# A planned kernel of memory attention and a gated layer on one core: one block's loads issued earlier, casts, output stores and weight sums put elsewhere in the plan

## The chip, the core and the metric

The kernel runs on one core of one Trainium2 chip. The metric is the time of one execution on the device in microseconds. Beside it stand profiles: one execution recorded by the hardware profiler, with a span from the first to the last instruction. The engines are PE (TensorE), DVE (VectorE), ACT (ScalarE), POOL (GpSimd) and SP (SyncE, which issues the loads and stores); each works through its own queue in order.

## What is computed

Attention with a compressive memory, over 4 batches, 8 heads, 576 positions and 64 channels, and behind it a gated feed-forward layer on its 2304 x 512 result:

```python
local = softmax(scale * q @ k.T, causal) @ v
mem_out = (phi(q) @ M_prev) / (phi(q) @ z_prev + 1e-6)
x = (g * mem_out + (1 - g) * local)          # 2304 tokens x 512
gate = x @ w_gate                            # 512 -> 1536
out = (silu(gate) * (x @ w_val)) @ w_out     # 1536 -> 512
```

## The kernel before

Every product runs on fp32 data split in two parts: a high part, cast to fp32r by ACT (`...h`), and a low part, what is left of it, by DVE (`...l`). A product is then three matmuls (high x high, high x low, low x high).

The attention fills about the first 183 us and leaves its result in DRAM as `xdh` and `xdl`. The tokens are then taken as three blocks of 768 (`ORDER`, line 30). Each block is multiplied with the 12 slices of 128 columns (f = 0 to 11) of `w_gate` and `w_val`. Except for the first three slices of block one, a slice and a block together form a **unit**: Strassen's seven products p1 to p7 in the order of `STEPS` (line 37), each of six matmuls of 128 x 384. `chain` (line 869) holds what follows each product. The products go by turns into two PSUM banks (`ring`, line 737), and several add up in the same bank, so that a product two steps later has to wait until the bank was read: ACT copies p1, p6 and p7 out (`zp`, `zh`, `zv`; in blocks two and three `zpw` and `zvw`), and DVE adds to these when it reads p2, p5 and p4 (`zg`, `zv`, `zh`), with a SiLU on ACT behind p2 and p4. After p3, DVE forms the two results of the unit (`use`).

The seven products need sums of the four quarters of a block's input. `sums` (line 755) makes them: `begin` issues the loads of the first two quarters (`load(0)`, `load(1)`, each one DMA from `xdh` into `xr` or `yr` and one from `xdl` into `xm` or `xt`, `ym` or `yt`), `add(n)` adds high and low part on DVE and, for n = 0 and 1, issues the loads of quarter n + 2, and four more DVE instructions make the sums. Each load is told to wait for the DVE instruction that was the last in program order when it was written (line 766). For block two the tiles are called x, for block three y. `high` and `low` (lines 784 and 787) then split a sum, `yp7h` and `yp7l` for p7 of block three. Quarters needed unmixed are loaded by `direct` (line 749).

The weights come as 64-bit numbers and are unpacked in thirds (`third`, line 248) by ACT, POOL and DVE; `operands` (line 708) makes the sums of weights for the next unit: `tt` (DVE), `th` and `bh` (ACT), `tl` and `bl` (DVE). The last output products of block one (`lower`, line 804) run between the products of the following unit.

The order is written out by hand. `seven` (line 898) runs one unit: after product n come the entries of `plan[n]`, then, if n is in `away_at`, one entry of `leave`, then one `lower`. The entries of `leave` are `away` (line 814): ACT scales one finished bank of block one's output into a tile `pt` of the pool `tmp`, and SP stores it. PE, ACT, DVE and POOL keep program order (`queued`, line 83); DMAs are put in SP's queue by the framework's scheduler, by when their data and memory are ready.

The part around the change goes as follows:
- block one, f = 3 to 11, in the loop from line 947 (`left` is 11 - f);
- first lone unit (line 1019): block two, f = 11, with block one's last six `lower`s; three `away`s after n = 3, 5 and 6;
- second lone unit (line 1043): block two, f = 10; the splits of block three's sums are in its plan, and three `away`s after n = 0, 2 and 4;
- third lone unit (line 1055): block three, f = 10; sums of results that are kept for later (`some_sums`);
- the pools `xr3p` and `tmp` are released and `tp` is opened in their room (lines 1056 to 1059);
- fourth lone unit (line 1079): block three, f = 11; the operands for f = 0 are in its plan;
- then ten pairs of units, f = 0 to 9, in which blocks two and three take turns product by product (line 1131), and from line 1198 the output products of these two blocks.

`tees(r)` (line 1061) makes sums of `w_out` for the output products, six rounds: two loads into `w2` (called `w` in the trace), four subtractions on POOL into `tq` and a store to `tdr`. There are two `w2` and two `tq`. Round 0 is written in the fourth lone unit after n = 0, round 1 + f in pair f after n = 1; the pool `tp` is released at the pair behind the last round, and `p3a` is opened there.

Of the kernel before, what the change touches and what calls it, by code (L numbers as in the profile page):

```python
# [29 lines left out]
ORDER = (0, 768, 1536)  # L30
# [15 lines left out]
def attention_moe(ctx: ExitStack, tc: tile.TileContext, qt, kt_, v, m, beta, wg, wv, wo, out):  # L46
# [123 lines left out]
    xs = {p: [near.tile([128, 2, N2], F32R, name=f"x{p}{part}") for part in "hl"] for p in STEPS}  # L170
# [530 lines left out]
    xr3p = tc.alloc_tile_pool(name="xr3", bufs=1, side="right", reuse_waits="tile")  # L701
# [53 lines left out]
    def sums(t0, pool_, name, here=False):  # L755

        got = rot(pool_, f"{name}r", [128, 4, 2, N2], F32, 1)
        a21, a22, a11, a12 = (got[:, n] for n in range(4))
        s1, s = (rot(pool_, f"{name}{n}", [128, 2, N2], F32, 1) for n in "tm")
        two = (s, s1)  # L760
        mix = dict(p6=s, p7=a11, p5=s1, p3=a12)

        def load(n):
            for dst, src in ((got[:, n], xdh), (two[n % 2], xdl)):
                ld = SP.dma_start(dst, block(src, t0, *AT[n]))
                follow(ld, last[DVE], "the loads that come before go first", mybir.DependencyClass.Sync)

        def add(n):
            if here:
                h, l = (x.bitcast(F32) for x in xs[("p7", "p4", "p1", "p2")[n]])  # L770
                dve.tensor_tensor(got[:, n], h, l, op=ALU.add)
                return
            dve.tensor_tensor(got[:, n], got[:, n], two[n % 2], op=ALU.add)
            if n + 2 < 4:
                load(n + 2)

        tt = lambda out, a, b, op: (lambda: dve.tensor_tensor(out, a, b, op=op))
        work = [lambda n=n: add(n) for n in range(4)] + [
            tt(s1, a21, a22, ALU.add), tt(s, s1, a11, ALU.subtract), tt(a12, a12, s, ALU.subtract),
            tt(a11, a11, a21, ALU.subtract),  # L780
        ]
        return lambda: (load(0), load(1)), work, mix
# [56 lines left out]
    ring2 = ring(*banks[0:2])  # L839
# [58 lines left out]
    def seven(w, x, bank, use, down, plan, away_at, hold=hold):  # L898
        step = chain(w, x, bank, use, hold)
        for n in range(7):  # L900
            step(n)
            if n == 0:
                halves()
            for work in plan[n]:
                work()
            if leave and n in away_at:
                leave.pop(0)()
            if n and down:
                down.pop(0)()
# [6 lines left out]
    def stored(b, f):  # L916
        def use(i, g, v):
            weighed(g, v)
            kept_u[b, f, i] = g
            if (f % 2, i) != (0, 1):  # L920
                keep(b, {(0, 0): "p1", (1, 0): "p2", (1, 1): "p4"}[f % 2, i], f, g)
            if i and (b, f ^ 1, 0) in kept_u:
                sums_due.extend(mixed(b, f))
        return use
# [21 lines left out]
    before, arrive, ready = None, [], {}  # L946
    for f in range(NF):
        plain, left = f < PLAIN, NF - 1 - f
        plan = [[] for _ in range(4 if plain else 7)]
        if left == 0:  # L950
            again(0)
        for k, i in zip((0, 1, 2) if plain else (2, 4, 6), slots_of[f]):
            plan[k].append(lambda i=i: third(i))
        plan[3].append(lambda: low_part(dve))
        if NF > f + 1 >= PLAIN:
            ready[f + 1], work = operands(f + 1)
            if plain:
                work = [work[0] + work[1], work[2] + work[3], work[4] + work[5], work[6]]
            for k, some_ in enumerate(work):
                plan[k] += some_  # L960
        for k, work in arrive:
            plan[k] += work
        arrive = []
        if plain:
            if f == 0:
                _, due, mix = sums(first, tmp, "x", True)
                for k, some_ in enumerate(((0,), (1,), (2, 4), (3,))):
                    plan[k] += [due[i] for i in some_]
            if f == 1:
                for k in range(3):  # L970
                    plan[k].append(due[5 + k])
                for k, p in ((0, "p5"), (2, "p6")):
                    plan[k] += spreads(mix, ("h", p))
                    plan[k + 1] += spreads(mix, ("l", p))
            if f == PLAIN - 1:
                plan[0] += spreads(mix, ("h", "p3"))
                plan[2] += spreads(mix, ("l", "p3"))
                arrive = [(0, spreads(mix, ("h", "p7"))), (1, spreads(mix, ("l", "p7")))]
        if left in (5, 4, 3):
            if left == 5:  # L980
                begin, due, mix = sums(ORDER[1], tmp, "x")
                begin()
            plan[5].append(due[5 - left])
        if left == 2:
            plan[5].append(due[3])
        if left == 1:
            for k, work in zip((1, 3, 5), due[4:]):
                plan[k].append(work)
            begin3, due3, mix3 = sums(ORDER[2], xr3p, "y")
            plan[6].append(begin3)  # L990
        if left == 0:
            for k, work in zip((0, 1, 5), due3):
                plan[k].append(work)
            plan[2].append(due[7])
            plan[3] += spreads(mix, ("h", "p6"))
            plan[4] += spreads(mix, ("l", "p6"), ("h", "p7"))
            plan[6] += spreads(mix, ("l", "p7"))
            arrive = [
                (1, spreads(mix, ("h", "p5"))), (2, spreads(mix, ("l", "p5"))),
                (3, spreads(mix, ("h", "p3"))), (4, spreads(mix, ("l", "p3"))),  # L1000
            ]
        down = [] if before is None else [lambda j=j, before=before: lower(*before, j) for j in range(2 * nj)]
        if plain:
            u = eight(f, down, plan)
        else:
            u = [None, None]
            seven(ready[f], xs, ring2, lambda i, g, v: weigh(u, i, g, v), down, plan, ())
        before = (f, u)
# [3 lines left out]
    LATE = NF - 1, NF - 2  # L1012
    plan = [[] for _ in range(7)]
# [13 lines left out]
    def holds(b):  # L1027
        def hold2(name):
            if name in ("zp", "zv"):
                return rot(z2p, f"{name}w", [128, N2], F32, 3 if name == "zp" else 2)  # L1030
            return rot(z2p, f"{name}{b}", [128, N2], F32, 4)
        return hold2
# [3 lines left out]
    ring3 = ring(*banks[2:4])  # L1036
    both = slice(0, 2)
    plan = [[] for _ in range(7)]
    for k, p in ((0, "p6"), (1, "p7"), (2, "p5"), (4, "p3")):
        plan[k].append(high(mix3, p, both, x3))  # L1040
    for k, p in ((1, "p6"), (2, "p7"), (3, "p5"), (6, "p3")):
        plan[k].append(low(mix3, p, both, x3))
    seven(ready[LATE[1]], xs, ring2, stored(0, LATE[1]), [], plan, (0, 2, 4), holds(0))

    def some_sums(n=1):
        for _ in range(n):
# [5 lines left out]
    plan = [[] for _ in range(7)]  # L1052
# [22 lines left out]
    plan = [[] for _ in range(7)]  # L1075
    for k, some_ in enumerate(work):
        plan[k] += some_
    plan[0].append(tees(0))
    seven(ready[LATE[0]], x3, ring3, stored(1, LATE[0]), [], plan, (), holds(1))

    NC = 3
# [45 lines left out]
                load_t(n + 2)  # L1127

    p3a = None
    T_AT = range(0, 5)  # L1130
    for f in range(NF - 2):
        plan = [[] for _ in range(14)]
        if f + 2 < NF - 2:
            again(f + 2)
        w, w1 = w1, None
        for k in (1, 5, 7, 9):
            plan[k].append(some_sums)
        if f + 1 < NF - 2:
            w1, work = operands(f + 1)
            for k, some_ in enumerate(work):  # L1140
                plan[2 * k] += some_
        if f in T_AT:
            plan[1].append(tees(1 + f))
        if f == T_AT[-1] + 1:
            tp.release()
            p3a = tc.alloc_tile_pool(name="p3a", bufs=1, reuse_waits="tile")
        if f == NF - 4:
            load_t(0)
            load_t(1)
        if f == NF - 3:  # L1150
            for n in range(U_AHEAD):
                load_u(n)
            for c in range(NC):
                plan[(0, 2, 4)[c]].append(lambda c=c: split_t(0, c))
            for k, n in ((7, 0), (11, 1), (13, 2)):
                plan[k].append(lambda n=n: prep(n))
        chains = [chain(w, xs, ring2, stored(0, f), holds(0)), chain(w, x3, ring3, stored(1, f), holds(1))]
        for n in range(14):
            chains[n % 2](n // 2)
            for work in plan[n]:  # L1160
                work()
# [110 lines left out]
```

## Time and profile before

| | |
|---|---|
| median of 3 runs | 604.1 us (603.87 to 605.07) |
| the profiled execution, its own time | 605.62 us |
| its span | 603.7 us |
| PE, busy | 587.5 us, 97% of the span |
| DVE, busy | 482.6 us, 80% |
| ACT, busy | 392.0 us, 65% |
| POOL, busy | 240.1 us, 40% |
| mean granted clock of PE | 0.992 of full speed |
| chain that ended last | PE 89%, DVE 4%, DMA 2%, ACT 2% |

All instructions that go through the helpers carry line 88, so groups are told apart by the names of the tiles, written out<-in, with the numbers of buffers left out. In a list of instructions the columns are start in us, duration in us, engine, line, operation, tiles and shapes; brackets give the idle time of the engine just before and what ended it. The bank names `s` and `tr` are PSUM.

### The profile page before, as it was taken

The page shows a single profiled execution, that of the slowest core. Times are in us where ns is not written, and L with a number is a line of the kernel's source. Part 1 is how long each engine was busy: PE and PEld are TensorE (multiplying, and loading weights), DVE is VectorE, ACT ScalarE, POOL GpSimd, SP SyncE. Part 2 cuts the span into 40 slices and gives each one's busy share as a digit, 9 for nine tenths or more (in the row PEclk, how much of TensorE's full clock was granted, in tenths as well). Part 3 has the DMA queues.
Part 4 walks back from the last instruction along what each step waited for, and adds up shares of the span by engine and source line. Part 5 has one row for each costly group of instructions (what it writes and reads, how often), then busy time and mean ns, then how long its engine had stood idle before and what let it go on. Part 6 is the DMA issues. An engine that isn't in the chain of part 4 may idle for free.

```text
span 603.7 us, 11980 instructions
## 1 busy us (share of the span) xinstructions
PE 587.5 (97%) x4118; PEld 542.7 (90%) x4118; DVE 482.6 (80%) x1161; ACT 392.0 (65%) x895; POOL 240.1 (40%) x285
## 2 busy tenths in 40 slices
PE   5999999999999999999998999999999999999997
PEld 4887878888888999999987899999999999999997
DVE  7799999999988998898977779676777766975671
ACT  7798998899886777777643744444444446656631
POOL 6999999999963334334420038200000000000000
PEclk9899999999999999999998999999999999999999
DMA  8446856657327446698548589835434426997852
GB/s 239 127 159 180 272 174 196 234 177 243 121 103 283 176 158 229 194 347 265 168 148 305 177 288 331 291 136 177 144 115 141 143 106 198 340 396 231 273 177 73
DMA packets 66091, 124.25 MB, mean 206 GB/s; under 512 B 8304, under 2 KB 37360, under 8 KB 66032
## 3 DMA queue, kind: packets, MB, share of 16 engines
q1 hardware_dynamic: 65744, 123.21, 61.3%
q8 instruction: 32, 0.52, 0.4%
q10 hardware_dynamic: 288, 0.30, 0.2%
q14 instruction: 27, 0.22, 0.1%
HBM read 80.23 MB, written 43.25 MB: 205 GB/s over the span
## 4 chain that ended last, share of the span: by engine, by line
PE 89%; DVE 4%; DMA 2%; ACT 2%; issue 1%; POOL 1%; SPq 0%; DVEq 0%
PE s L88 58%; PE tr L88 31%; DMA kr<-in_kt_dram 1%; DMA ym<-xdl 1%; DVE tt L88 1%; DMA up<-zh 1%; DVE zg L88 1%; DVE xr L88 0%; DVE bl L88 0%; DVE zh L88 0%; DVE tl L88 0%; POOL ps L88 0%; ACT g L88 0%; ACT we L88 0%; POOL kl L88 0%
## 5 line engine op out<-in xcount | busy, mean ns | idle before, releaser
L88 POOL TENSOR_SCALAR pl<-pl,rs,og 128x384 f32<-128x384 f32 (+1 forms) x64 | 54.3, 862 | 5.4 <-DVE rs L88 5.0
L88 POOL TENSOR_SCALAR we<-we 128x512 f32<-128x512 f32 x32 | 25.2, 789 | 74.4 <-ACT we L88 74.2
L88 ACT ACTIVATE zh<-zh 128x384 f32<-128x384 f32 x33 | 17.3, 525 | 52.0 <-DVE zh L88 51.9
L88 PE MATMUL tr<-g,vp 128*64 128x320 f32 (+4 forms) x448 | 48.8, 361 | 0.3 <-ACT g L88 0.3
L88 PEld LDWEIGHTS tr<-g,vp 128*64 128x64 f32 x448 | 29.3, 137 | 18.1 <-issue 2.5
L88 ACT ACTIVATE pl<-pl,mx 128x384 f32<-128x384 f32 (+1 forms) x64 | 42.4, 665 | 4.6 <-DVE mx L88 3.8
L88 PE MATMUL s<-kh,qh 64*128 64x128 f32 (+4 forms) x160 | 36.3, 381 | 4.3 <-ACT kh L88 4.2
L88 DVE CUSTOM_DVE_ANT_0 pl<-s,maskp 128x384 f32<-128x384 f32 (+1 forms) x64 | 38.3, 618 | 1.2 <-PE s L88 0.8
L88 ACT ACTIVATE zg<-zg 128x384 f32<-128x384 f32 x33 | 17.3, 524 | 25.0 <-DVE zg L88 24.5
L88 ACT COPY g<-tr 128x384 f32<-128x384 f32 (+1 forms) x60 | 30.0, 525 | 4.7 <-PE tr L88 4.7
L88 ACT ACTIVATE ps<-ps,mx 128x128 f32<-128x128 f32 (+1 forms) x64 | 28.6, 454 | 6.2 <-DVE mx L88 6.1
L88 POOL TENSOR_SCALAR ps<-ps,rs,og 128x128 f32<-128x128 f32 (+1 forms) x64 | 32.0, 515 | 1.4 <-DVE rs L88 1.0
L88 POOL TENSOR_TENSOR tq<-w 128x256 f32<-128x256 f32 x12 | 11.2, 956 | 53.8 <-DMA w<-wdw 52.1
L88 PE MATMUL s<-kl,qh 64*128 64x128 f32 (+4 forms) x160 | 31.2, 327 | 1.4 <-POOL kl L88 1.4
L88 PE MATMUL s<-kh,ql 64*128 64x128 f32 (+4 forms) x160 | 31.1, 326 | 0.0
L88 DVE COPY g<-tr 128x384 f32<-128x384 f32 (+2 forms) x60 | 29.8, 515 | 1.5 <-PE tr L88 1.4
L88 PE MATMUL tr<-ident,pl 128*128 128x128 f32 x210 | 29.9, 282 | 0.1
L88 PEld LDWEIGHTS tr<-ident,pl 128*128 128x128 f32 x210 | 23.4, 143 | 6.5 <-issue 3.5
L88 DVE TENSOR_TENSOR tl<-tt,th 128x512 fp32r<-128x512 f32 x38 | 28.0, 737 | 0.0
L88 ACT CAST th<-tt 128x512 fp32r<-128x512 f32 x38 | 23.7, 623 | 6.6 <-DVE tt L88 5.5
L88 DVE TENSOR_TENSOR zvw<-s,zvw 128x384 f32<-128x384 f32 x23 | 12.7, 556 | 18.5 <-PE s L88 17.2
L88 PEld LDWEIGHTS s<-kh,qh 64*128 64x128 f32 (+1 forms) x160 | 19.1, 195 | 8.5 <-POOL qh L88 4.1
(492 smaller groups left out, 2293.0 us busy)
## 6 DMA issues: line engine op xcount, KB each, us to landing
ur<-up SPq DMA_DIRECT2D x42, 384.0 KB, 4.8
up<-zg SPq DMA_DIRECT2D x36, 192.0 KB, 2.5
wraw<-in_wg_dram SPq DMA_DIRECT2D x12, 512.0 KB, 4.5
wraw<-in_wv_dram SPq DMA_DIRECT2D x12, 512.0 KB, 4.8
wraw<-in_wo_dram SPq DMA_DIRECT2D x12, 512.0 KB, 5.0
qr<-in_qt_dram SPq DMA_DIRECT2D x15, 384.0 KB, 3.2
vp<-in_v_dram SPq DMA_DIRECT2D x16, 320.0 KB, 4.8
wr<-wdr SPq DMA_DIRECT2D x10, 512.0 KB, 3.7
```

Of the source, the lines that this page charges most:

```text
L88: ins = getattr(eng, name)(*args, **kw)
```

## The change

Four edits of the plan, in the same function:
- `begin` of block three's sums moves from the end of unit f = 10 to the end of unit f = 8 of block one (`left` 1 to `left` 3).
- In the second lone unit the casts of p7 and p5 move one step back, from after n = 1 and 2 to after n = 2 and 3, and their low parts with them. The three `away`s leave this unit; they fall to the third lone unit, whose `away_at` (0, 2, 4) had nothing to take.
- Round 0 of `tees` leaves the fourth lone unit; rounds 0 to 5 are written in pairs 0 to 5.
- With that the release of `tp` and the opening of `p3a` move from pair 5 to pair 6.

```diff
@@ -981,13 +981,14 @@
             plan[5].append(due[5 - left])
+        if left == 3:
+            begin3, due3, mix3 = sums(ORDER[2], xr3p, "y")
+            plan[6].append(begin3)
         if left == 2:
             plan[5].append(due[3])
         if left == 1:
             for k, work in zip((1, 3, 5), due[4:]):
                 plan[k].append(work)
-            begin3, due3, mix3 = sums(ORDER[2], xr3p, "y")
-            plan[6].append(begin3)
@@ -1036,11 +1037,11 @@
-    for k, p in ((0, "p6"), (1, "p7"), (2, "p5"), (4, "p3")):
+    for k, p in ((0, "p6"), (2, "p7"), (3, "p5"), (4, "p3")):
         plan[k].append(high(mix3, p, both, x3))
-    for k, p in ((1, "p6"), (2, "p7"), (3, "p5"), (6, "p3")):
+    for k, p in ((1, "p6"), (3, "p7"), (4, "p5"), (6, "p3")):
         plan[k].append(low(mix3, p, both, x3))
-    seven(ready[LATE[1]], xs, ring2, stored(0, LATE[1]), [], plan, (0, 2, 4), holds(0))
+    seven(ready[LATE[1]], xs, ring2, stored(0, LATE[1]), [], plan, (), holds(0))
@@ -1075,7 +1076,6 @@
-    plan[0].append(tees(0))
     seven(ready[LATE[0]], x3, ring3, stored(1, LATE[0]), [], plan, (), holds(1))
@@ -1127,7 +1127,7 @@
-    T_AT = range(0, 5)
+    T_AT = range(0, 6)
@@ -1140,7 +1140,7 @@
         if f in T_AT:
-            plan[1].append(tees(1 + f))
+            plan[1].append(tees(f))
```

## Rows read from the trace of the kernel before

**Rows 1.** Windows: span; busy PE, PEld, DVE, ACT, POOL; PEclk; DMA share, GB/s.

```profile
311.06:328.12 17.06, 13.40 (x62) 12.11 (x60) 10.13 (x18) 5.43 (x12) 0.00 (x0) 0.90 0.96 331
328.12:339.68 11.56, 11.56 (x62) 10.79 (x60) 9.91 (x19) 6.49 (x14) 0.00 (x0) 1.00 0.20 71
339.68:348.11 8.43, 7.88 (x44) 7.23 (x43) 5.76 (x9) 6.41 (x12) 0.00 (x0) 1.00 0.99 321
348.11:355.46 7.35, 7.35 (x44) 7.23 (x44) 5.29 (x10) 2.38 (x6) 0.00 (x0) 1.00 1.02 353
355.46:364.97 9.51, 7.87 (x43) 7.22 (x43) 8.15 (x12) 4.41 (x10) 7.54 (x9) 1.00 0.70 229
364.97:379.60 14.63, 14.63 (x86) 14.63 (x86) 13.31 (x22) 6.86 (x15) 12.71 (x15) 1.00 0.95 334
394.20:408.80 14.60, 14.60 (x85) 14.60 (x85) 10.44 (x22) 6.74 (x14) 0.00 (x0) 1.00 0.42 145
```

**Rows 2.** Waits of PE from 299 to 366: us in total, times, longest.

```profile
PE s L88 <- DVE zg L88: 3.7, 1, 3.7
PE s L88 <- DVE zvw L88: 1.1, 1, 1.1
PE s L88 <- ACT zh L88: 0.8, 2, 0.6
PE s L88 <- ACT zvw L88: 0.3, 1, 0.3
```

**Rows 3.** Timeline of PE, last unit of block one.

```profile
319.44 0.46 PE L88 MATMUL s<-xp7h,th 128*128 128x384 f32 x1 [3.66 <-DVE zg L88]
```

**Rows 4.** Timeline of DVE, same unit.

```profile
317.95 0.96 DVE L88 TENSOR_TENSOR yr<-yr,ym 128x768 f32<-128x768 f32 x1 [4.52 <-DMA ym<-xdl]
318.83 0.55 DVE L88 TENSOR_TENSOR zg<-s,zp 128x384 f32<-128x384 f32 x1
```

**Rows 5.** Windows, the slow stretch behind the stop (columns as in rows 1).

```profile
320.60:324.10 3.50, 3.50 (x12) 3.21 (x11) 3.03 (x4) 1.80 (x5) 0.00 (x0) 0.51 1.06 381
```

**Rows 6.** Windows, the unit of block one with f = 9.

```profile
288.00:299.50 11.50, 11.50 (x62) 10.61 (x61) 10.67 (x20) 8.68 (x17) 4.62 (x5) 1.00 0.46 154
```

**Rows 7.** Timeline of ACT, second lone unit.

```profile
343.07 0.82 ACT L88 CAST yp7h<-yr 128x768 fp32r<-128x768 f32 x1
343.80 0.47 ACT L88 COPY zh<-s 128x384 f32<-128x384 f32 x1
...
344.90 0.60 ACT L88 ACTIVATE pt<-tr 128x512 f32<-128x512 f32 x1
```

**Rows 8.** Timeline of SP's queue, second lone unit.

```profile
342.56 0.46 SPq L751 DMA_DIRECT2D yp2l<-xdl  x1
```

**Rows 9.** DMA issues: KB each, us to landing.

```profile
yp2l<-xdl SPq DMA_DIRECT2D x1, 384.0 KB, 5.8
```

**Rows 10.** Timeline of POOL, fourth lone unit.

```profile
357.27 1.45 POOL L88 TENSOR_TENSOR tq<-w 128x256 f32<-128x256 f32 x2 [52.09 <-DMA w<-wdw]
```

**Rows 11.** Groups by form, DVE, 355.4 to 364.9: busy us, mean ns, idle before.

```profile
L88 DVE TENSOR_TENSOR tt<-wr,tt 128x256 f32<-128x256 f32 x2 | 1.8, 896 | 0.0
L88 DVE TENSOR_TENSOR bl<-wr,bh 128x512 fp32r<-128x512 f32 x1 | 1.2, 1219 | 0.0
L88 DVE TENSOR_TENSOR tt<-wr 128x512 f32<-128x512 f32 x1 | 1.0, 979 | 0.0
```

**Rows 12.** Groups by form, DVE, 394 to 408.6.

```profile
L88 DVE TENSOR_TENSOR tt<-wr,tt 128x256 f32<-128x256 f32 x2 | 0.8, 418 | 0.0
L88 DVE TENSOR_TENSOR bl<-wr,bh 128x512 fp32r<-128x512 f32 x1 | 0.7, 684 | 0.0
L88 DVE TENSOR_TENSOR tt<-wr 128x512 f32<-128x512 f32 x1 | 0.7, 681 | 0.0
```

**Rows 13.** Timeline of SP's queue, second and third lone unit.

```profile
344.30 3.16 SPq L817 DMA_DIRECT2D out_dram<-pt  x3
...
352.47 2.07 SPq L1065 DMA_DIRECT2D w<-wdw  x4
```

## The prediction, written before the changed kernel was run

> **What bounds the kernel now.** I read the page first: TensorE (PE) is busy for 97% of the span and the chain that ended last is 89% PE, so only places where PE stops or runs slowly can give time. Then the windows table, cut where one unit of seven products ends and the next begins [rows 1]. The last unit of block one and the first lone unit hold the same matmuls (seven products and six `lower` calls each), yet take 17.06 and 11.56 us: 5.50 us too much in the first. The three lone units after it hold seven products and nothing else; the middle one takes 7.35 us with PE busy throughout, its neighbours 8.43 and 9.51: 1.08 and 2.16 us too much. Together 8.74 us, the most that this change can win. Then PE's waits over the same stretch [rows 2]: 3.7 us for DVE's `zg`, 1.1 us for DVE's `zvw`, 0.8 us in two waits (the longer 0.6) for ACT's `zh`, 0.3 us for ACT's `zvw`. Nothing else stops PE there.
>
> **Part 1, the third block's first loads.** In the last unit of block one PE stands still for 3.66 us at 319.44 until `zg` has been read from its bank [rows 3]. DVE reads it late because it is in order and has `add(0)` of block three in front; that sat idle for 4.52 us until `ym` had landed, and `zg` came right after, at 318.83 [rows 4]. The load was issued only at the end of the unit before, some 5 us ahead of its landing. Then a second price: from 320.60 to 324.10 the granted clock is 0.51, the lower of the two levels (1.2 GHz), after 1.00 up to the stop [rows 5]; only this stop came before it, the clock is 1.00 in the lone units that have only shorter waits [rows 1]. Wait and slow stretch are together the 5.50 us.
>
> The change issues the four loads two units earlier, 23.1 us by the unit length of 11.56 us. They need some 6 us, so they are there long before `add(0)`. What they meet: in the window from 288 to 299.5 the DMA engines are busy for 0.46 of the time [rows 6], against 0.96 in the unit that they leave [rows 1]; 1.6 MB fits, and I cost it at nothing. The loads wait for the last DVE instruction of their unit, and behind them in SP's queue stand stores of finished weights and reloads that are used a unit or more later. In the old place the queue becomes shorter by four issues, so block two's `xp1h`, `xp2h`, `xp2l` start earlier.
>
> What is late next: DVE is free at 313.43 (317.95 less 4.52), `add(0)` takes 0.96 and `zg` 0.55 [rows 4], so the bank is read at 314.9; PE asks for it at 315.78 (319.44 less 3.66) [rows 3]. That is 0.8 us of cover; a wait shorter than that on DVE would not show. `add(1)` and `add(2)` need loads issued when `add(0)` and `add(1)` are done; they have several microseconds more and fewer neighbours than now. Gain: 5.5 us, bounds 3.7 (the wait alone, if the clock fell anyway) and 5.5.
>
> **Part 2, the order on ACT in the second lone unit.** ACT ran the cast `yp7h` (0.82 us) and only behind it the bank copy `zh`, and PE waited for that copy; the same pattern, with `yp5h` and the output scaling `pt` (0.60) ahead of the copy `zvw`, makes the second wait [rows 7]. Afterwards the cast of p7 stands behind the copy of p6, that of p5 behind that of p7, and the three output scalings are gone to the next unit. `zh` can then start at 343.07, where the cast starts now, and ends 0.7 us earlier than now, more than PE's wait of 0.2 to 0.3. Behind it come `yp7h` (0.82) and `zvw` (about 0.47), which ends at about 344.8; PE, by then the whole 1.08 us earlier, comes to that bank at about 344.9. Both waits go, the second with 0.1 to 0.2 us to spare. The casts themselves move by less than 1 us and are used a unit later. What is late next is a load: `yp2l`, issued at 342.56, lands 5.8 us later, at 348.4 [rows 8, 9]; it is read with the second matmul of p2, some 1.2 us after the third unit's start at 348.11 [rows 1], and would be wanted at 348.2. The three output stores that now share the engines with it leave, so I take back only 0.1 us: gain 1.0 us, bounds 0.5 and 1.08.
>
> The output scalings and their stores land in the third lone unit, where ACT is busy for 2.38 of 7.35 us [rows 1]; 1.8 us more fits between its copies, each copy still a few tenths ahead of PE. Cost nothing; if the cover failed, one scaling ahead of a copy would cost up to 0.6 us.
>
> **Part 3, the sums of w_out on GpSimd (POOL).** In the fourth lone unit POOL runs the first subtractions `tq` [rows 10], and DVE's operand work is slow there: 979 ns for a `tt` of 512 columns, 1219 for `bl`, 896 for a `tt` of 256 [rows 11]; two pairs later, with POOL idle [rows 1], the same take 681, 684 and 418 [rows 12]. One `tt`, one `bl` and two short ones stand ahead of `zvw`: 0.30 + 0.54 + 2 x 0.48 = 1.8 us, more than the 1.1 us for which PE waits for it [rows 2]. That wait goes. Of the 0.6 us for `zh` only 0.3 goes (that copy stands behind the cast of `tt`, which comes 0.30 us sooner). The unit's 2.16 us are 0.46 more than its two waits (1.1 + 0.6), 0.2 to 0.25 of restart for each. Gain: 2.16 us less the rest of the one wait (0.3) and its restart (0.25), so 1.6 us.
>
> But does the change move POOL's work out of this unit? Its place in the plan doesn't hold it: POOL's queue holds nothing else by then, and it runs all six rounds as fast as their loads come (12.71 us of the first pair [rows 1]). What holds it is the memory: `w2` and `tq` take over the room of `tmp`, with the output tiles `pt` in it. Now the last `pt` store is issued at about 347.5 and the `w` loads start at 352.47, 5.0 us later [rows 13]; POOL starts at 357.27, another 4.8 us on [rows 10]. In the change the last `pt` is written some 5.4 us into the third lone unit and its store issued 0.4 later; plus 9.8 us is 15.6 us, 8.2 us after the fourth lone unit begins. That unit then lasts 9.51 - 1.6 = 7.9 us: POOL starts just behind it. The first pair has POOL beside it already and PE 14.63 of 14.63 us busy; the second, which gets some 9 us of it, has nothing else new. Later allocations have over 60 us of room.
>
> A rule speaks against this. What the row shows first: in the first pair POOL is busy for 12.71 us and DVE for 13.31, in an equal pair without POOL DVE for 10.44, and PE never waits in either [rows 1]. The Trainium skill, page "SBUF — State Buffer", section "Who interferes with whom", says that a DVE instruction with two SBUF inputs contends with a GpSimd one that reads SBUF, and that the port pair is locked for a whole instruction. As far as DVE slows beside POOL, the trace agrees; by the rule at its fullest the moved work would stop DVE for its whole length, which the last rival prices.
>
> **The sum.** 5.5 + 1.0 + 1.6 = 8.1 us. The profiled execution took 605.62 us around a span of 603.7, 1.5 above the median of 604.1; the gains lie inside the span, so 597.5 for such an execution and 596.0 on the median.
>
> **The rivals.**
> - POOL comes as early as now, because its loads depend on their place in SP's queue and not on `pt`. For it: the loads of the second round too ran far ahead of their place in the plan. Against it: no `w` load starts before the stores are out. The fourth unit keeps 9.51 us: 604.1 - 6.5 = 597.6. Chance 0.11.
> - A new wait takes back 1 to 2 us: `yp2l` and its neighbours late for the third lone unit, or output scalings ahead of copies. For it: the small margins above. Against it: less traffic at that time. 597.0 to 598.0. Chance 0.07.
> - The loads are issued early but the stop forms again (DVE behind another load in that unit). Only 2.6 us are won: 601.5. Against it: `add(0)` is all that stood idle there. Chance 0.04.
> - Slower: POOL locks DVE in full in the two first pairs. DVE's 10.44 us and POOL's 12.71 would make 23.2 us in a pair of 14.6, 8.5 too many, and some 3.5 in the second: 596.0 + 12 = 608. It decides as soon as DVE's work with its stops exceeds a pair's length by more than the two products of cover that alternating chains give. Against it: by the same sum the first pair would be late now, and PE has no wait in it [rows 1]. Chance 0.02. It is what the Trainium skill's rule on that page, taken at its fullest, would give.
>
> **How the numbers follow.** My forecast, all three parts, has 0.74; two in a hundred go to causes I don't see. The least is 604.1 - 8.74 = 595.4, and runs of one kernel differ by about 0.6 us: low 594.8. The first two rivals reach to 598.0; with that spread, high 598.6. About 0.2% (1.2 us) is what a measurement of this kernel tells from no change. All cases but the last rival and half of the unseen give over 2 us: faster 0.96, same 0.02, slower 0.02.
>
> **What would show it.** Right: no wait of PE over 0.5 us between 300 and 360; the granted clock 1.00 in the last unit of block one, which takes 11.6 us; the lone units 7.4, 7.4 and 7.9 us; the `yr` loads near 290; POOL's first `tq` in the first pair. Wrong: a wait at `zg` that stays, a clock of 0.5 without a stop before it, or `tt` of 512 columns at 0.9 us in the fourth lone unit.

## Result and the profile after

The changed kernel takes 598.01 us, median of 4 runs (597.62 to 599.15), against 604.38 us (603.87 to 605.07) for the kernel before beside it: ratio 0.9897, 95% interval 0.988 to 0.9914, 6.4 us faster. The forecast was 596.0 (594.8 to 598.6): right in direction and within its range, 2.0 us too low. The profiled execution took 598.1 us with a span of 596.3.

Windows of the changed kernel, cut at the first matmul of each unit: last unit of block one, four lone units, pairs 0 and 1 (columns as in [rows 1]; below are those of before):

```profile
309.73:321.29 11.56, 11.56 (x62) 10.79 (x60) 8.84 (x16) 5.50 (x12) 0.00 (x0) 1.00 0.88 286
321.29:333.47 12.18, 12.09 (x62) 10.64 (x60) 11.01 (x20) 6.28 (x14) 0.00 (x0) 1.00 0.35 126
333.47:340.81 7.34, 7.34 (x43) 7.34 (x42) 5.54 (x9) 4.69 (x8) 0.00 (x0) 1.00 0.99 329
340.81:348.27 7.46, 7.46 (x43) 7.24 (x43) 5.39 (x11) 4.13 (x9) 0.00 (x0) 1.00 0.90 325
348.27:357.47 9.20, 7.86 (x43) 7.21 (x43) 7.84 (x12) 4.40 (x10) 6.04 (x7) 1.00 0.67 226
357.47:372.10 14.63, 14.63 (x86) 14.63 (x86) 13.27 (x22) 6.70 (x15) 11.87 (x14) 1.00 0.98 335
372.10:386.70 14.60, 14.60 (x86) 14.60 (x85) 9.71 (x19) 6.83 (x15) 3.46 (x5) 1.00 0.92 308
```

| unit | before | after | difference | forecast |
|---|---|---|---|---|
| last of block one | 17.06 | 11.56 | -5.50 | -5.5 |
| first lone | 11.56 | 12.18 | +0.62 | 0 |
| second lone | 8.43 | 7.34 | -1.09 | -1.08 |
| third lone | 7.35 | 7.46 | +0.11 | +0.1 |
| fourth lone | 9.51 | 9.20 | -0.31 | -1.6 |
| pairs 0 and 1 | 29.23 | 29.23 | 0 | 0 |
| sum | | | -6.17 | -8.1 |

The missing 1.93 us stand in two rows: 1.3 us in the fourth lone unit, where little was won, and 0.6 in the first, which no edit touches. The waits of PE from 298 to 359 say the same for the fourth: the waits of [rows 2] for `zg` and in the second lone unit are gone, these two are left, and both lie in the fourth lone unit.

```profile
PE s L88 <- DVE zvw L88: 1.1, 1, 1.1
PE s L88 <- ACT zh L88: 0.3, 1, 0.3
```

**First lone unit.** Timeline of DVE, then of SP's queue:

```profile
312.03 0.95 DVE L88 TENSOR_TENSOR yr<-yr,ym 128x768 f32<-128x768 f32 x1
312.89 0.55 DVE L88 TENSOR_TENSOR zg<-s,zp 128x384 f32<-128x384 f32 x1
...
321.04 0.96 DVE L88 TENSOR_TENSOR yr<-yr,ym 128x768 f32<-128x768 f32 x1 [1.43 <-DMA ym<-xdl]
```

```profile
312.52 0.46 SPq L751 DMA_DIRECT2D xp2h<-xdh  x1
313.08 0.41 SPq L765 DMA_DIRECT2D yr<-xdh  x1
313.53 0.47 SPq L765 DMA_DIRECT2D ym<-xdl  x1
```

`add(0)` runs at 312.03 without waiting (before, it sat idle for 4.52 us [rows 4]). But `add(2)` at 321.04 now sits idle for 1.43 us: its `ym`, issued at 313.53 behind four loads of block two, lands 7.4 us later. What stands behind it on DVE comes late, and two weight loads of PE wait for it: one for a bank that `zg` reads, one for the low part `ul` that the unit's first `lower` needs. In the kernel before neither wait is there. From the waits of PE's weight loads in this unit:

```profile
PEld s L88 <- DVE ul L88: 0.5, 1, 0.5
PEld s L88 <- DVE zg L88: 0.3, 1, 0.3
```

**Second lone unit.** On ACT each cast now stands behind a bank copy:

```profile
336.86 0.46 ACT L88 COPY zh<-s 128x384 f32<-128x384 f32 x1
337.22 0.84 ACT L88 CAST yp7h<-yr 128x768 fp32r<-128x768 f32 x1
337.95 0.48 ACT L88 COPY zvw<-s 128x384 f32<-128x384 f32 x1
338.32 0.84 ACT L88 CAST yp5h<-yt 128x768 fp32r<-128x768 f32 x1
```

**Fourth lone unit.** SP's queue ahead of it, and POOL's first subtraction:

```profile
345.34 1.35 SPq L817 DMA_DIRECT2D out_dram<-pt  x2
347.51 0.33 SPq L914 DMA_DIRECT2D up<-zg  x1
347.89 0.92 SPq L1066 DMA_DIRECT2D w<-wdw  x2
```

```profile
351.36 1.89 POOL L88 TENSOR_TENSOR tq<-w 128x256 f32<-128x256 f32 x2 [47.51 <-DMA w<-wdw]
```

The first two `w` loads go out 1.2 us after the output stores have been issued, not 5.0. The last two of these stores have not landed then: issued at 345.34 and 346.36, they take 4.1 and 3.7 us, to 349.44 and 350.06. The second pair of `w` loads, at 350.14, did wait for a store; from the waits of SP's queue between 340 and 372:

```profile
SPq L1066 <- DMA out_dram<-pt: 0.7, 1, 0.7
```

POOL's first subtraction needs only the first load, so POOL begins 3.1 us into the fourth lone unit, not behind it (before: 1.8 us into it [rows 10]). DVE's groups by form in that unit (last two numbers: mean ns, idle before): only the long `tt`, which begins at 351.10, 0.26 us ahead of POOL's start, became short (979 before [rows 11]); its 0.30 us agree with the 0.31 that the unit won. The last row has one of its two inputs in PSUM; it runs at 355.73, beside POOL.

```profile
L88 DVE TENSOR_TENSOR tt<-wr,tt 128x256 f32<-128x256 f32 x2 | 1.8, 895 | 0.0
L88 DVE TENSOR_TENSOR bl<-wr,bh 128x512 fp32r<-128x512 f32 x1 | 1.2, 1212 | 0.0
L88 DVE TENSOR_TENSOR tt<-wr 128x512 f32<-128x512 f32 x1 | 0.7, 683 | 0.0
...
L88 DVE TENSOR_TENSOR zvw<-s,zvw 128x384 f32<-128x384 f32 x1 | 0.5, 545 | 0.0
```

### The profile page after: what moved, and what is told of

It reads as the page before. It is cut to its first block, busy times and chain, and to the rows that moved or that the text cites. A ratio compares the mean times of both kernels' runs of the same rounds, so it can differ in the third digit from the quotient of the medians.

```text
span 596.3 us, 11984 instructions
## 1 busy us (share of the span) xinstructions
PE 584.6 (98%) x4118; PEld 540.1 (91%) x4118; DVE 480.5 (81%) x1161; ACT 391.6 (66%) x895; POOL 240.9 (40%) x285
## 4 chain that ended last, share of the span: by engine, by line
PE 88%; DVE 5%; DMA 3%; ACT 1%; issue 1%; POOL 1%; SPq 0%; DVEq 0%
PE s L88 58%; PE tr L88 31%; DMA ym<-xdl 1%; DMA qr<-in_qt_dram 1%; DVE zg L88 1%; DVE tt L88 1%; DMA up<-zh 1%; DVE zh L88 0%; DVE xr L88 0%; POOL ps L88 0%; DVE bl L88 0%; DVE tl L88 0%; ACT g L88 0%; DVE xp7l L88 0%; ACT we L88 0%
## 5 line engine op out<-in xcount | busy, mean ns | idle before, releaser
L88 POOL TENSOR_SCALAR we<-we 128x512 f32<-128x512 f32 x32 | 27.8, 869 | 72.0 <-ACT we L88 71.8
```

The source lines that it names most:

```text
L88: ins = getattr(eng, name)(*args, **kw)
```

## The experiments

Unit lengths are read as above. The runs stand on two chips; the kernel before took 603.5 us (median of 11) beside the early loads alone, the casts alone, the waiting loads and the second loads early, and 603.92 us (median of 7) beside the other four. A single run settles unit lengths, not totals.

### The early loads alone

The kernel before with only the move of `begin3`:

```diff
+        if left == 3:
+            begin3, due3, mix3 = sums(ORDER[2], xr3p, "y")
+            plan[6].append(begin3)
...
-            begin3, due3, mix3 = sums(ORDER[2], xr3p, "y")
-            plan[6].append(begin3)
```

> The kernel before with the first edit alone: block three's first four loads two units earlier. Theory (the stop at zg and the slow stretch behind it are the whole 5.50 us, and the follow-up loads of block three now land too late, which costs the next unit 0.6 us): the last unit of block one takes 11.56 us at a granted clock of 1.00, the first lone unit 12.2, the lone units after it 8.43, 7.35 and 9.51 as before; time 604.4 - 4.9 = 599.5 us. Rival (the 0.6 us in the first lone unit come from the other edits): first lone unit 11.56, time 598.9 us.

Measured: 599.21 us (598.76 to 601.49), ratio 0.9937 (0.9918 to 0.9956). Windows of the last unit of block one and of the first lone unit:

```profile
309.11:320.67 11.56, 11.56 (x62) 10.79 (x61) 9.19 (x16) 5.52 (x12) 0.00 (x0) 1.00 0.89 299
320.67:332.49 11.82, 11.82 (x62) 10.70 (x61) 10.64 (x20) 6.29 (x14) 0.00 (x0) 1.00 0.34 123
```

In the profiled executions the whole 5.5 us come from this edit, and so does the loss in the first lone unit, though smaller here (0.26 us): DVE idles 1.06 us for `ym`. The other units are those of before (8.43, 7.36, 9.47). The totals say less than the 5.24 us of the two units: by the interval of the ratio the edit saves 2.7 to 4.9 us. One of the 11 executions of the kernel before that stand beside it had a mean clock of 1.000 and took 602.59 us, the shortest of them; 3.5 us at 0.51 [rows 5] would lower that mean by 0.003, so the slow stretch behind the stop does not come in every execution.

The run also bears on what holds POOL's loads. SP's queue in this kernel, then the row of the kernel before that stands just ahead of its `w` loads [rows 13]:

```profile
344.91 0.32 SPq L914 DMA_DIRECT2D up<-zs  x1
345.29 2.74 SPq L1066 DMA_DIRECT2D w<-wdw  x4
```

```profile
352.09 0.33 SPq L914 DMA_DIRECT2D up<-zs  x1
```

In both the `w` loads start 0.38 us after the last `up<-zs`, a store of one of the third lone unit's kept sums: the four loads stand right behind it in an in-order queue. But these two kernels alone can't tell the queue from the memory. By issue and time to landing, the last output store lands at 352.42 in the kernel before (issued at 347.12, 5.3 us) and at 345.23 here, 0.05 and 0.06 us ahead of the first `w` load. Other kernels tell them apart: in the changed kernel the first pair starts 0.38 us after another store, `up<-zg`, and 2.2 us before the last output store lands; with the casts alone it starts 0.37 us after `up<-zs` (350.99) and 1.0 us before that landing (351.97). So the first pair of loads, on which POOL's start hangs, is held by its place in the queue. The second pair is held by the memory, as the wait of 0.7 us in the changed kernel shows. Why the scheduler gives the loads that place is not shown.

### The casts alone

The kernel before with only the casts of p7 and p5 one step back; the three output scalings stay in the second lone unit:

```diff
-    for k, p in ((0, "p6"), (1, "p7"), (2, "p5"), (4, "p3")):
+    for k, p in ((0, "p6"), (2, "p7"), (3, "p5"), (4, "p3")):
...
-    for k, p in ((1, "p6"), (2, "p7"), (3, "p5"), (6, "p3")):
+    for k, p in ((1, "p6"), (3, "p7"), (4, "p5"), (6, "p3")):
```

> The kernel before with only the casts of p7 and p5 (and their low parts) one step back in the second lone unit; the output scalings stay there. Theory (a cast ahead of a bank copy is what PE waits for): the wait for zh (0.27 us) goes, and of the wait for zvw (0.29 us) at most what the output scalings make stays; the unit takes 7.4 to 7.8 us in place of 8.43. Rival (the output scalings are the cause): it stays at 8.2 us or more. The time moves by under 1.1 us either way and is not what this run is for.

Measured: 604.14 us, one run; second lone unit 7.70 us:

```profile
338.92:346.62 7.70, 7.58 (x43) 7.26 (x42) 5.69 (x9) 6.17 (x12) 0.00 (x0) 1.00 0.99 324
```

Of the 1.09 us the casts bring 0.73; the 0.36 left to the moved scalings are a difference between two kernels, no run moves them alone.

### POOL held back in two ways

First the loads: the changed kernel, with the loads of round 0 told to wait for the last DVE instruction ahead of them in program order:

```diff
-            SP.dma_start(w2[:, j], wdw[2 * r + j])
+            ld = SP.dma_start(w2[:, j], wdw[2 * r + j])
+            if r == 0:
+                follow(ld, last[DVE], "after the lone units", mybir.DependencyClass.Sync)
```

> The changed kernel, with the two loads of round 0 of the w_out sums told to wait for the last DVE instruction of the fourth lone unit. Theory (POOL's subtractions beside DVE's two-input work are what makes the fourth lone unit long): POOL starts in the first pair, tt of 512 and 256 columns take 0.68 and 0.42 us, the wait for zvw (1.1 us) goes, the wait for zh stays at 0.3, the unit takes 7.9 us in place of 9.20; time 598.0 - 1.3 = 596.7 us. Rival 1 (DVE is slow there for another reason): the unit stays near 9.2, time 598.0. Rival 2 (POOL's work then holds up the first two pairs): the unit gets shorter and the pairs longer than 14.63 us, time 598 or more.

Measured: 597.16 us (596.76 to 597.84), ratio 0.9892 (0.9879 to 0.9904). Windows of the fourth lone unit and pairs 0 and 1, then DVE's groups in the fourth lone unit:

```profile
348.40:356.28 7.88, 7.62 (x43) 7.30 (x43) 5.89 (x12) 4.38 (x10) 0.00 (x0) 1.00 0.37 119
356.28:370.90 14.62, 14.62 (x86) 14.62 (x85) 12.72 (x21) 6.82 (x15) 8.60 (x9) 1.00 0.73 231
370.90:385.50 14.60, 14.60 (x85) 14.60 (x85) 10.75 (x19) 6.82 (x15) 10.62 (x14) 1.00 0.93 305
```

```profile
L88 DVE TENSOR_TENSOR tt<-wr,tt 128x256 f32<-128x256 f32 x2 | 0.8, 422 | 0.0
L88 DVE TENSOR_TENSOR bl<-wr,bh 128x512 fp32r<-128x512 f32 x1 | 0.7, 686 | 0.0
...
L88 DVE TENSOR_TENSOR zvw<-s,zvw 128x384 f32<-128x384 f32 x1 | 0.6, 558 | 0.5 <-PE s L88 0.5
```

The unit takes 7.88 us, where 7.9 was forecast for it, and the pairs that take POOL's work are no longer. The two loads of round 1, which were not told to wait, still go out in the unit, at 349.69, just behind the landing of the last output store (issued at 346.47, 3.2 us). The total shows little of it; in this run `ym` was later and the first lone unit took 12.60 us.

Then POOL's work alone: the changed kernel with its loads left as they are, and the same wait on the first subtraction.

```diff
-                pool.tensor_tensor(tq[:, n], a, b, op=ALU.subtract)
+                ins = pool.tensor_tensor(tq[:, n], a, b, op=ALU.subtract)
+                if r == n == 0:
+                    follow(ins, last[DVE], "after the lone units", mybir.DependencyClass.Sync)
```

> The changed kernel with the loads of the w_out sums left early and only the first subtraction on POOL told to wait for the last DVE instruction of the fourth lone unit. Theory (POOL's own work beside DVE costs the 1.3 us): fourth lone unit 7.9 us, as where the loads wait; 596.7 us. Rival (the loads' traffic delays something in that unit): 9.2 us, 598 us.

Measured: 596.74 us, one run; first and fourth lone unit:

```profile
320.46:333.72 13.26, 12.12 (x61) 10.67 (x60) 11.27 (x20) 6.29 (x14) 0.00 (x0) 1.00 0.32 114
348.45:356.31 7.86, 7.60 (x44) 7.28 (x44) 5.90 (x12) 4.38 (x10) 0.00 (x0) 1.00 0.56 187
```

7.86 us with the loads nearly as early as in the changed kernel (348.66 and 350.41): POOL's subtractions beside DVE are the cause, not the traffic. That the total hits the forecast of 596.7 is chance, since the first lone unit is 1.08 us longer here than in the changed kernel. DVE instructions with two SBUF inputs get longer beside POOL, the costly ones by about half a microsecond (`tt` 895 against 422 ns, `bl` 1212 against 686), but not all: a `bl` of 256 columns at 356.20, beside POOL too, takes 476 against 414. `zvw<-s,zvw`, with one input in PSUM, takes 545 ns beside POOL and 558 without. The Trainium skill, page "SBUF — State Buffer", section "Who interferes with whom", draws the line at the same place: outside the 2-port modes a DVE instruction with at most one SBUF input doesn't contend with GpSimd, and one with two contends with a GpSimd instruction that reads SBUF; the rows agree.

### The w_out sums back at their old places

The changed kernel with round 0 written in the fourth lone unit again:

```diff
+    plan[0].append(tees(0))
     seven(ready[LATE[0]], x3, ring3, stored(1, LATE[0]), [], plan, (), holds(1))
...
-    T_AT = range(0, 6)
+    T_AT = range(0, 5)
...
-            plan[1].append(tees(f))
+            plan[1].append(tees(1 + f))
```

> The changed kernel with the six rounds of w_out sums back at their old places in the plan (round 0 in the fourth lone unit, the pool released at pair 5). Theory (the place in the plan does nothing; memory that comes free sets the loads, and the moved output stores set that): fourth lone unit 9.2 us and POOL's first subtraction some 3 us into it, as in the changed kernel; 598.0 us. Rival (the move is worth what the unit lost, 0.3 us, by its place): 9.5 us, POOL 1.8 us into the unit.

Measured: 597.67 us, one run; fourth lone unit 9.22 us, POOL's first subtraction 3.3 us into it.

```profile
347.80:357.02 9.22, 7.86 (x44) 7.22 (x43) 7.86 (x12) 4.40 (x10) 5.72 (x7) 1.00 0.71 225
```

So this edit of the change does nothing by itself. The early loads alone (9.47 us) and the casts alone (9.63) don't give the 0.31 us of that unit either, which leaves the moved output stores: in the changed kernel the `w` loads start 0.4 us before the unit and not 3.0. No run moves these stores alone.

### The second loads early too

The changed kernel with the high parts of quarters 3 and 4 (`yr`) loaded together with the first four:

```diff
-        return lambda: (load(0), load(1)), work, mix
+        return lambda: (load(0), load(1), ahead and (load(2, (0,)), load(3, (0,)))), work, mix
...
-                load(n + 2)
+                load(n + 2, (1,) if ahead else (0, 1))
```

> The changed kernel, with the high parts of block three's third and fourth quarter loaded together with the first four loads (their room is free then), so that only two loads follow in the last unit of block one in place of four. Theory (add(2) is late because ym, the follow-up load, lands 7.4 us after its issue behind the loads of xp1 and xp2): DVE's wait for ym of 1.43 us shrinks or goes, ul comes in time, the first lone unit takes 11.6 to 11.9 us in place of 12.18; time 597.4 to 597.7 us. Rival (DVE has too much work there, whatever the loads): the unit stays at 12.2, time 598.0.

Measured: 600.77 us (599.86 to 602.75), ratio 0.9955 (0.9939 to 0.9972): slower than the changed kernel. The first lone unit is back at 11.54 us (11.6 to 11.9 expected; `add(2)` still waits 0.72 us for `ym`, which doesn't show), but unit f = 10 has a new stop. The profiled execution is the slowest of the six, 602.75 us. Its window of that unit and the slow stretch in it, PE's stop, and what ACT waited for there:

```profile
298.66:314.68 16.02, 13.36 (x61) 12.07 (x60) 12.22 (x22) 6.60 (x13) 3.31 (x3) 0.89 0.45 168
305.50:309.00 3.50, 3.50 (x12) 3.16 (x11) 3.50 (x7) 2.08 (x5) 1.10 (x1) 0.51 0.20 75
```

```profile
304.28 0.44 PE L88 MATMUL s<-xp6h,th 128*128 128x384 f32 x1 [2.66 <-ACT zp L88]
```

```profile
303.21 0.66 ACT L88 ACTIVATE we<-wraw 128x512 f32<-128x512 f32 x1 [2.82 <-DMA wraw<-in_wo_dram]
```

The last raw weight load `wraw` stands behind the y loads. With four ahead of it (the changed kernel) it is issued at 290.91 and lands 7.4 us later, at 298.3; ACT comes to it at 299.80. With six it is issued at 293.85, lands 9.3 us later, and ACT, then the bank copy `zp`, then PE wait. So the collision in unit f = 9 that the prediction cost at nothing had 1.5 us of cover in the changed kernel, no more.

### Both causes mended

The changed kernel with the wait on the `w` loads, and the two `yr` loads in the middle of unit f = 9:

```diff
-            tt(a11, a11, a21, ALU.subtract),
+            tt(a11, a11, a21, ALU.subtract), lambda: (load(2, (0,)), load(3, (0,))),
...
-                load(n + 2)
+                load(n + 2, (1,) if ahead else (0, 1))
...
         if left == 2:
             plan[5].append(due[3])
+            plan[3].append(due3[8])
...
+            if r == 0:
+                follow(ld, last[DVE], "after the lone units", mybir.DependencyClass.Sync)
```

> The changed kernel with both causes of the lost time mended: the first weight loads of the w_out sums wait for the last DVE instruction of the lone units, and the high parts of quarters 3 and 4 of block three are loaded in the middle of unit f = 10 (behind the last raw weight load), not behind add(0) and add(1). Theory (two separate causes): fourth lone unit 7.9 us, first lone unit 11.55 us in place of 12.2 to 12.6, unit f = 10 stays at 11.56 without the stop at zp, everything else as in the changed kernel: 598.0 - 1.3 - 0.6 = 596.1 us. Rival (the load in unit f = 10 meets the last weight load or its store, whatever its place): f = 10 longer by 1 us or more, 597 us or more. Rival (the low part alone is as late as before, since the other late loads hold it up): first lone unit 12.2, 596.7 us.

(The text says unit f = 10; `left == 2` is f = 9. The loads went out at 292.82, behind `wraw` at 290.00, which is what was meant.) Measured: 595.77 us (595.09 to 596.24), ratio 0.9866 (0.9849 to 0.9883), against 0.9897 for the changed kernel: by the ratios 1.9 us less (their intervals just touch), by the units 2.0 us. Unit f = 10 and the four lone units:

```profile
297.29:308.87 11.58, 11.58 (x62) 10.68 (x61) 11.58 (x21) 6.43 (x13) 3.96 (x3) 1.00 0.51 185
...
320.43:331.99 11.56, 11.56 (x62) 10.79 (x61) 9.91 (x19) 6.48 (x14) 0.00 (x0) 1.00 0.21 77
331.99:339.32 7.33, 7.33 (x43) 7.33 (x42) 5.54 (x9) 4.69 (x8) 0.00 (x0) 1.00 0.99 329
339.32:346.75 7.43, 7.43 (x44) 7.25 (x43) 5.39 (x11) 4.13 (x9) 0.00 (x0) 1.00 0.90 326
346.75:354.62 7.87, 7.64 (x44) 7.32 (x44) 5.89 (x12) 4.35 (x10) 0.00 (x0) 1.00 0.35 120
```

Both losses are gone and no new stop is there. Over the runs, the first lone unit goes with DVE's idle time before `add(2)`:

| kernel | `ym` from issue to landing | DVE idle | first lone unit |
|---|---|---|---|
| both mended | 6.2 | 0 | 11.56 |
| early loads alone | 7.0 | 1.06 | 11.82 |
| w_out sums put back | 7.2 | 1.23 | 12.01 |
| changed kernel | 7.4 | 1.43 | 12.18 |
| `w` loads wait | 7.8 | 1.85 | 12.60 |
| POOL waits | 8.4 | 2.48 | 13.26 |

Each unit but the first row's is longer than 11.56 by the idle time less 0.8 us; the run with the second loads early fits too (0.72 us, no loss). The kernel of the next section doesn't (1.54 us, 12.66): there PE also stops for 0.46 us for `zg`, which DVE reads right behind `add(2)`. In all rows but the first the loads ahead of `ym` are the same, in the same order; why it lands 7.0 us after its issue in one and 8.4 in another stays open.

### A shorter stop

The kernel before with `begin3` one product earlier:

```diff
+            begin3, due3, mix3 = sums(ORDER[2], xr3p, "y")
+            plan[5].append(begin3)
             for k, work in zip((1, 3, 5), due[4:]):
                 plan[k].append(work)
-            begin3, due3, mix3 = sums(ORDER[2], xr3p, "y")
-            plan[6].append(begin3)
```

> The kernel before with block three's first four loads issued one product earlier (ahead of the last DVE instruction of the sums in unit f = 10), so that PE's stop at zg should be roughly half as long, 1.5 to 2.5 us in place of 3.66. Theory (the lower clock follows a stop of PE of this size too; the stop of 2.66 us at zp in the run with all high parts early was followed by a mean clock of 0.89): the unit takes 11.56 + stop + 1.5 to 1.9 us, 14.6 to 16 us, with rows at 0.5. Rival (the clock falls only behind a stop of more than about 2.5 us): 11.56 + stop, clock 1.00. If the stop does not shrink, the loads are held by other loads in the queue and not by their issue.

Measured: 602.75 us, one run. The last unit of block one and PE's longest stop in it:

```profile
309.89:324.09 14.20, 11.95 (x61) 10.60 (x60) 8.59 (x15) 5.43 (x12) 0.00 (x0) 1.00 1.00 340
```

```profile
316.85 0.44 PE L88 MATMUL s<-xp7h,th 128*128 128x384 f32 x1 [2.25 <-DVE zg L88]
```

The unit is 2.64 us longer than 11.56: 2.25 us of the stop, and 0.4 us in which PE is not recorded as waiting (a weight load waits 0.33 us for `zv`). The clock is 1.00 throughout, as the rival said. With the high parts early, a stop of 2.66 us came before 3.5 us at 0.51, the lower level, and the unit was 2.66 + 1.80 us longer; in the kernel before, one of 3.66 cost 5.50 in all [rows 1, 3]. These are one execution each. At which length of a stop the clock falls, and whether it falls every time, these runs don't say.

## Why the prediction was right, and where its sizes were off

- **In all.** The time lies in the stated range, but its upper part was there for the first two rivals, and both came in part: POOL stayed in the fourth lone unit, and a new loss of 0.62 us came. Of the stated signs, the `yr` loads near 290 (288.79) and the clock held; "no wait of PE over 0.5 us" (1.1 for `zvw`), the fourth lone unit of 7.9 us (9.20) and POOL's first `tq` in the first pair did not.
- **Part 1, right in size; one sentence of it failed.** Wait and slow stretch went together, 5.50 of 5.5 us, and the bank is read before PE asks for it. (The four loads of before were issued from 312.61 on, 1.6 us into the unit with the stop, not at the end of the unit before; the gain does not hang on it.) What failed is "`add(1)` and `add(2)` need loads issued when `add(0)` and `add(1)` are done; they have several microseconds more and fewer neighbours than now". Before, `ym` for `add(2)` was issued at 319.40 and wanted at 326.35, 6.95 us later. After, it was issued at 313.53 and wanted at 321.04 - 1.43 = 319.61, 6.08 us later. The issue hangs on `add(0)`, which came 5.9 us earlier, but the use came 6.7 us earlier, since the slow stretch behind the stop, which lay between the two, went too. And four loads of block two now stand directly ahead of it, and it takes 7.4 us to land in place of 6.4. So it has less time and needs more: +0.62 us in this profile, +0.26 to +1.70 over the runs.
- **Costing the collision in unit f = 9 at nothing** held, with 1.5 us to spare. The working had missed the load with the least room: `wraw`, which stands behind the four loads, is used 8.9 us after its issue, and two more loads in front of it made it late.
- **Part 2, right:** 1.09 us won in the second lone unit, and 0.11 lost in the third, where the weight load of PE waits 0.2 us for `yp2l`, as foreseen. The output scalings cost nothing there.
- **Part 3, mis-sized: 0.31 us in place of 1.6.** The price of POOL beside DVE was right (7.88 and 7.86 us against a forecast of 7.9 with POOL out of the unit). The step that failed is "What holds it is the memory". The 5.0 us before the `w` loads were read as the time in which the room of the `pt` tiles comes free, for all of them. It holds the second pair, which in the changed kernel starts at 350.14, 0.08 us after the last output store has landed. The first pair, with which POOL begins, stood in SP's queue behind an `up` store, and in the changed kernel it starts 2.2 us before that landing. This was in the main the first rival, "its loads depend on their place in SP's queue and not on `pt`" (597.6); I had given it 0.11, and its argument against, that no `w` load starts before the stores are out, was true of both readings. Its unit of 9.51 us came to 9.20.
- **The other rivals.** A new wait came, 0.62 us in place of 1 to 2, and not where it was looked for. The stop did not form again in the changed kernel. POOL did not lock DVE in full: the pairs keep 14.63 and 14.60 us.
- **The sum.** 8.1 - 6.17 = 1.93 us: 1.29 from part 3, 0.62 from the first lone unit, 0.02 from part 2. The medians differ by 6.37; the kernel before was 0.28 us above the 604.1 of the forecast. The gap to 596.0 is 8.1 - 6.37 + 0.28 = 2.0 us.

## What to carry to other kernels

A load that follows an instruction moves with it, but so does the moment at which its data are wanted: after taking out a stall, work out issue-to-use anew for every later load of the chain, since the stall and the slow stretch behind it were hiding them. When a transfer starts late, look at the row just ahead of it in its queue and at the landing of what held its memory: in the kernel before both fell within 0.05 us of each other, and only a kernel in which they fall apart could tell which one it was. And an instruction's place in a written plan holds nothing on an engine that has nothing else to do; to keep work out of a stretch, give it a wait.

## What was not expected of the hardware

A stop of PE of 2.25 us left the granted clock at 1.00, one of 2.66 us was followed by 3.5 us at 0.51, and the unit was 1.80 us longer than the stop alone makes it; one execution of each. And one load of 384 KB behind the same neighbours landed between 7.0 and 8.4 us after its issue in five kernels; that spread alone moved the first lone unit by 1.44 us (11.82 to 13.26).
